# A two-layer attention and MLP kernel: dummy matmuls on a built-in constant, short ones behind the first transposes, b2 loaded later, new order lists

## The chip, the cores and the metric

The kernel runs on one core of a Trainium2 chip. The metric is the device time of one execution in microseconds, from the median of several runs; smaller is better. A profiled execution is a further run of the same program, for which every instruction's start and duration are recorded.

Five engines work side by side, each through its own list of instructions in order: TensorE (PE; its weight loads are shown as PEld), VectorE (DVE), ScalarE (ACT), GpSimd (POOL) and SyncE (SP), which here only issues DMAs. An engine that waits for a semaphore holds up everything behind the waiting instruction in its own list.

## The reference

The input `x` is one sequence of 2048 tokens of width 512. The same block, with the same weights, is applied twice:

```python
x = x + A(layernorm(x), wqkv, wo)              # linear attention, 32 heads of 16
x = x + B(layernorm(x), w1, b1, w2, b2)        # B normalises once more, then an MLP of width 1792
# A: q, k, v = x @ wqkv;  phi(t) = where(t > 0, t + 1, exp(t)) + 1e-6
#    kv = phi(k)^T v ;  z = sum over tokens of phi(k)
#    o = phi(q) kv / (phi(q) z + 1e-6) ;  result o @ wo
# B: gelu_tanh(layernorm(x) @ w1 + b1) @ w2 + b2
```

All inputs are bf16. The sum over tokens in `kv` and `z` means that no token's attention output is known before all 2048 tokens have been through the K projection.

## The kernel before, in words

**Tiling.** The 2048 tokens are four chunks of 512, each of four tiles of 128 (tile st = 4 * chunk + k). In layer 0 the chunks are taken in the order `C0=(3, 0, 1, 2)`, so tile 12 is the first one. For a tile the front does: statistics of the row (`stats`, `aggr`, or for tile 13 `sum` and `sq` on ScalarE), then `norm` (or `cen`, a subtraction of the mean, with the scale `ysc` applied afterwards), a transpose, and the K projection `K0_st` (four matmuls of 512 columns, L838), whose result goes through `exp`, `relu`, `min` and `phi` into `pk`. `G0_st` (L939) sums y^T phi(k) in four PSUM banks over all tiles. Q projections are `Q0_c_k` (L856, L869). Tiles 12 to 15 and tile 1 are transposed by TensorE (`PTA0_st`, L783, four matmuls of 128 columns, copied out of PSUM by ScalarE as `tcA0_st`, L793); all other tiles of layer 0 by DMA transposes that SP issues (`TA0_st`, L770).

**Loads.** `x0`, `x1` and `x2` are the first chunk's tiles 12, 13, and 14 with 15 (128, 128 and 256 KB). `wk0` and `wk1` are the halves of the K weights (256 KB each; `wk1` goes through ScalarE's queue, all others through SP's), `wq` the Q weights (512 KB). `xc0`, `xc1`, `xc2` are the chunks 0, 1, 2 (512 KB each, tiles 0 to 3, 4 to 7, 8 to 11; L638). `b1` and `b2` are biases; `b2` (128 KB) is broadcast over the partitions. `wv`, `wo`, `w1`, `w2` are issued by GpSimd once all of layer 0's first transposes are done.

**Order.** The program is a graph of named operations. `CONF["ORDER"]` holds one list of names for each engine, and the engine's instructions go out in exactly that order: `Scheduler.run` only ever takes the head of a list, `assign_waits` adds the semaphore waits that the graph's dependences need, and `play` emits them. `Scheduler.run` also carries a small model of times (how long a DMA takes, when the bus is free); it decides buffer slots, and the lists were settled with it. It doesn't reorder a list.

The lines that matter at the start are these:

```python
ones = G.op("dve", lambda e: e.memset(onesm[:], 1.0), 480, writes=["onesm"], ...)       # L641
def warm(e):                                                                            # L678
    for n in [D] * cf["N_WARM"] + [P]:
        ins = e.matmul(bank(wu, n), lhsT=onesm[:, 0:P], rhs=onesm[:, 0:n], start=True, stop=True)
```

`warm` is TensorE's first operation: seven dummy matmuls of 512 columns and one of 128, whose result nobody reads. It reads `onesm`, a tile that VectorE fills. The first entries of three lists of before are:

```
pe   warm PTA0_12 PTA0_13 K0_12 K0_13 PTA0_14 Q0_3_0 Q0_3_2 PTA0_15 K0_14 ... G0_14_0 Q0_3_3 PTA0_1 K0_0 K0_1 ...
dve  ones statsA0_12 aggrA0_12 cenA0_12 ... mink0_15 normA0_1 aggrA0_2 phik0_15 statsA0_8 normA0_2 ...
sp   x0 x1 wk0 x2 wq xc0 xc1 xc2 TA0_0 TA0_3 TA0_2 TA0_8 TA0_4 b2 TA0_6 TA0_7 TA0_5 TA0_10 TA0_11 TA0_9 b1 Tb1 ...
```

Of the kernel before, what the change touches and what calls it, by code (L numbers as in the profile page):

```python
# [6 lines left out]
BF16 = mybir.dt.bfloat16  # L7
# [3 lines left out]
P = 128  # L11
# [99 lines left out]
class Scheduler:  # L111
# [12 lines left out]
    def run(self):  # L124
# [14 lines left out]
        for _ in g.ops:  # L139
# [38 lines left out]
            if e == "sp" or o.sem is not None:  # L178
                if o.name[0] == "T":
                    o.end = max(at + o.lat, bus + 1000.0 if bus > at + 300.0 else 0.0)  # L180
                else:
                    bus = max(at + (1300.0 if at < 1400.0 else 1700.0 if e == "pool" else 900.0), bus) + o.nbytes
                    o.end = bus + o.lat
            else:
                o.end = at + dur + o.lat
# [79 lines left out]
def assign_waits(graph, order, sems, dma_sems):  # L265
# [10 lines left out]
    while len(done) < total:  # L276
        moved = False
        for e in ENGINES:
# [43 lines left out]
    C0=(3, 0, 1, 2), N_WARM=7, ZC=(0, 3), LQ='sp', N_HALF=1, N_K=4, N_Q=3, P_Z0=6.15, N_PB=1, N_PT=8, P_DEN=-50.43,  # L322
# [4 lines left out]
            "warm PTA0_12 PTA0_13 K0_12 K0_13 PTA0_14 Q0_3_0 Q0_3_2 PTA0_15 K0_14 G0_12_0 Q0_3_1 K0_15 G0_13_0 "  # L327
            "G0_14_0 Q0_3_3 PTA0_1 K0_0 K0_1 G0_15_0 K0_3 G0_0_0 K0_2 Q0_0_2 Q0_0_0 G0_1_0 K0_8 Z0_3 K0_4 G0_2_0 "
            "K0_6 G0_3_0 Q0_0_3 K0_7 K0_5 G0_4_0 K0_10 K0_11 Z0_0 K0_9 Q0_1_2 Q0_1_3 Z0_1 Q0_0_1 Q0_1_0 Z0_2 "
            "G0_5_0 G0_6_0 D0_0_3 D0_0_0 G0_7_0 Q0_1_1 D0_0_1 G0_8_0 D0_0_2 G0_9_0 G0_10_0 G0_11_0 G0_11_2 G0_11_1 "  # L330
            "D0_1_0 Q0_2_0 G0_11_3 KV0_0 KV0_1 D0_1_1 ZR0 KV0_2 KV0_3 Q0_2_1 D0_1_2 M0_0 M0_1 M0_2 M0_3 Q0_2_2 "
            "WO0_0_0 WO0_0_1 WO0_0_2 WO0_0_3 D0_1_3 WO0_1_0 WO0_2_0 WO0_3_0 Q0_2_3 WO0_4_0 WO0_7_0 WO0_6_0 PTB0_0 "
            "WO0_5_0 W10_0_5_0 W10_0_1_0 W10_0_9_0 W10_0_6_0 W10_0_2_0 W10_0_3_0 W10_0_12_0 W10_0_7_0 W10_0_0_0 "
            "W10_0_4_0 W10_0_13_0 W10_0_11_0 W10_0_8_0 W10_0_10_0 W20_0_0 W20_1_0 W20_0_7 W20_1_7 W10_0_9_1 "
            "W10_0_1_1 W10_0_7_1 W10_0_8_1 W10_0_5_1 W10_0_6_1 W10_0_12_1 W10_0_0_1 W10_0_13_1 W10_0_3_1 "
            "W10_0_11_1 W10_1_4_0 W10_1_13_0 W10_0_4_1 W10_1_11_0 W10_1_0_0 W10_1_3_0 W10_1_2_0 W10_0_2_1 "
            "W10_1_6_0 WO0_9_0 WO0_8_0 WO0_11_0 W10_1_5_0 W10_1_8_0 W10_1_10_0 WO0_10_0 W10_0_10_1 W10_1_1_0 "
            "W10_1_12_0 W10_1_7_0 W10_1_9_0 W20_7_0 W20_4_0 W20_7_7 W20_4_7 WO0_15_0 W20_5_0 W20_2_0 W20_5_7 "
# [24 lines left out]
            "reluq0_3_1 tcA0_1 expq0_3_1 expk0_0 reluk0_1 expk0_1 expq0_3_3 reluq0_3_3 normA0_8 expk0_3 expk0_2 "
            "normA0_6 reluk0_3 expq0_0_2 reluq0_0_2 reluq0_0_0 normA0_7 expk0_8 expk0_4 normA0_5 normA0_10 expk0_6 "
            "reluk0_6 expq0_0_0 expk0_7 expq0_0_3 reluk0_5 expk0_5 expk0_10 expk0_11 reluk0_11 reluk0_9 expk0_9 "
            "reluq0_1_2 expq0_1_2 expq0_1_3 expq0_0_1 reluq0_0_1 expq0_1_0 ln0_0_3 ln0_0_0 rec0_0_3 rec0_0_0 "
            "reluq0_1_1 ln0_0_1 rec0_0_1 expq0_1_1 ln0_0_2 rec0_0_2 ln0_1_0 b1c expq0_2_0 rec0_1_0 ln0_1_1 cpz0 "
            "rec0_1_1 cpm0_0 cpm0_1 cpm0_3 ln0_1_2 rec0_1_2 ln0_1_3 rec0_1_3 expq0_2_1 reluq0_2_1 expq0_2_3 "
# [159 lines left out]
def build_kernel(nc, A_x, A_wqkv, A_wo, B_x, B_w1, B_b1, B_w2, B_b2, out, conf=None, report=False):  # L528
# [5 lines left out]
    with ExitStack() as es:  # L534
# [48 lines left out]
        def bank(t, n=512):  # L583
            return ps[:, t.slot, 0:n]
# [62 lines left out]
        for h, q in enumerate(("sp", "act")):  # L647
            dma(q, lambda e, h=h: e.dma_start(wqkv[:, 2 * h:2 * h + 2, D:2 * D], wsrc[:, 2 * h:2 * h + 2, D:2 * D]), [f"wk_{h}"], prio=-99,
                name=f"wk{h}", kb=256, after=[ones] if q == "act" else ())
# [702 lines left out]
```

## Time and profile before

| | |
|---|---|
| runs | 331.65, 331.3, 328.13 us (median 331.3) |
| profiled execution, device time | 330.35 us |
| its span, first to last instruction | 328.6 us |
| PE busy | 322.0 us, 98% |
| DVE, ACT, POOL busy | 223.0 us (68%), 194.4 us (59%), 133.1 us (41%) |
| DMA | 20.37 MB, mean 62 GB/s |

The span is what the trace shows; 1.75 us of device time lie around it. A row of the timeline has the start, the duration, the engine, the line in the code, the operation, what it writes and reads, how many were merged into the row, and in brackets how long the engine had been idle before it and what ended that. A matmul's duration there includes its way through the array, so matmuls overlap; what a matmul costs TensorE is the distance from its start to the next one's.

### The profile page before, as it was taken

How to read it: one execution, taken by the hardware profiler on the slowest of the kernel's cores; microseconds unless marked ns; L12 is line 12 of the kernel's file. 1: busy time of each engine (PE TensorE's matmuls, PEld its weight loads, DVE VectorE, ACT ScalarE, POOL GpSimd, SP SyncE). 2: the span in 40 equal slices, each digit the busy share in tenths (PEclk: the TensorE clock that was granted, in tenths of full speed). 3: DMA queues.
4: the chain of work that ended last, by engine and by line, in shares of the span. 5: the costliest groups of instructions: out<-in, count | busy, mean ns of one | idle time of the engine just before them, and what ended most of it. 6: DMA issues, size and time to landing. Idle time of an engine off the chain costs nothing.

```text
span 328.6 us, 4769 instructions
## 1 busy us (share of the span) xinstructions
PE 322.0 (98%) x1716; PEld 159.1 (48%) x1716; DVE 223.0 (68%) x507; ACT 194.4 (59%) x334; POOL 133.1 (41%) x223
## 2 busy tenths in 40 slices
PE   7999999999999999999999999999999999999996
PEld 2444545476544444444444444448644444444444
DVE  4799599999794554575158899999989776100132
ACT  4898769783747055536984377878933452567200
POOL 3366646567447105533047725756903176000000
PEclk9999999999999999999999999999999999999999
DMA  6324593105404300312101110022044214200011
GB/s 231 152 49 98 121 358 149 18 16 97 49 0 66 80 16 3 64 32 48 34 16 32 35 32 0 2 49 50 18 96 99 48 33 97 64 0 2 16 48 64
DMA packets 47027, 20.37 MB, mean 62 GB/s; under 512 B 41948, under 2 KB 45532, under 8 KB 47004
## 3 DMA queue, kind: packets, MB, share of 16 engines
q1 hardware_dynamic: 45676, 15.09, 20.7%
q0 software_dynamic: 1056, 4.72, 4.1%
q8 instruction: 13, 0.21, 0.3%
q10 hardware_dynamic: 272, 0.26, 0.3%
q14 instruction: 10, 0.08, 0.1%
HBM read 8.00 MB, written 2.10 MB: 31 GB/s over the span
## 4 chain that ended last, share of the span: by engine, by line
PE 94%; DMA 2%; DVE 1%; ACT 1%; issue 0%; SPq 0%; ACTq 0%
PE ps L1119 30%; PE ps L1157 29%; PE ps L838 9%; PE ps L1087 8%; PE ps L856 5%; PE ps L971 4%; PE ps L939 3%; PE ps L869 2%; DMA wqkv<-in_A_wqkv_dram 1%; DMA t<-yb 1%; PE ps L1144 1%; PE ps L1063 1%; PE ps L1017 1%; PE ps L994 1%; PE ps L783 0%
## 5 line engine op out<-in xcount | busy, mean ns | idle before, releaser
L1125 ACT ACTIVATE gT<-ps,b1c 128x512 bf16<-128x512 f32 (+1 forms) x140 | 77.0, 601 | 53.8 <-PE ps L1119 53.3
L1119 PE MATMUL ps<-t,w 128*128 128x512 bf16 (+1 forms) x560 | 101.3, 336 | 0.4 <-issue 0.4
L1157 PE MATMUL ps<-w,gT 128*128 128x512 bf16 x434 | 97.3, 379 | 0.0
L1119 PEld LDWEIGHTS ps<-t,w 128*128 128x128 bf16 x560 | 54.6, 98 | 43.6 <-ACT t L793 1.2
L1157 PEld LDWEIGHTS ps<-w,gT 128*128 128x128 bf16 x434 | 42.5, 98 | 50.8
L808 ACT ACTIVATE eb<-ps 128x512 bf16<-128x512 f32 x56 | 32.5, 602 | 31.0 <-PE ps L838 25.6
L735 POOL TENSOR_TENSOR rstd<-veps,neghalf 128x1 f32<-128x1 f32 x64 | 37.8, 598 | 8.3 <-DVE veps L733 5.9
L1167 DVE TENSOR_TENSOR outb<-ps,xsb 128x512 bf16<-128x512 f32 x15 | 10.2, 683 | 40.2 <-PE ps L1157 38.7
L838 PE MATMUL ps<-wqkv,t 128*128 128x512 bf16 x128 | 33.6, 394 | 1.4 <-DMA t<-yb 0.7
L720 DVE BATCH_NORM_STATS2 stats<-xsb 128x6 f32<-128x512 f32 x48 | 32.0, 680 | 0.3
L1087 PE MATMUL ps<-gtb,t 128*128 128x512 bf16 x128 | 30.9, 379 | 0.0
L760 DVE TENSOR_SCALAR yb<-xsb,mv,rstd 128x512 bf16<-128x512 f32 x28 | 16.7, 602 | 13.6 <-POOL rstd L735 13.4
L733 POOL TENSOR_SCALAR veps<-mv 128x1 f32<-128x1 f32 x28 | 7.4, 276 | 43.7 <-DVE mv L722 43.0
L755 ACT ACTIVATE yb<-xsb,nmr,rstd 128x512 bf16<-128x512 f32 x20 | 15.7, 811 | 14.6 <-POOL nmr L752 14.6
L819 ACT ACTIVATE rb<-ps 128x512 bf16<-128x512 f32 x38 | 21.8, 601 | 0.2 <-PE ps L838 0.2
L821 DVE TENSOR_SCALAR eb<-eb 128x512 bf16<-128x512 bf16 x46 | 14.4, 325 | 10.1 <-ACT eb L808 10.0
L725 POOL TENSOR_SCALAR veps<-mv 128x1 f32<-128x1 f32 x32 | 8.8, 274 | 29.1 <-DVE mv L722 27.2
L838 PEld LDWEIGHTS ps<-wqkv,t 128*128 128x128 bf16 x128 | 12.3, 100 | 17.0 <-issue 1.7
L856 PE MATMUL ps<-wqkv,t 128*128 128x512 bf16 x80 | 20.3, 383 | 0.0
L1163 DVE TENSOR_TENSOR xsb<-ps,xsb 128x512 f32<-128x512 f32 x16 | 11.0, 688 | 13.2 <-PE ps L1157 13.1
L1087 PEld LDWEIGHTS ps<-gtb,t 128*128 128x128 bf16 x128 | 12.3, 98 | 15.1 <-DVE mv L722 0.5
L1104 POOL TENSOR_TENSOR xsb<-xsb,b2b 128x512 f32<-128x512 f32 x14 | 17.4, 1255 | 2.8 <-ACT yb L755 1.6
(103 smaller groups left out, 395.2 us busy)
## 6 DMA issues: line engine op xcount, KB each, us to landing
w<-in_B_w_dram POOLq DMA_DIRECT2D x4, 896.0 KB, 9.8
out_dram<-outb SPq DMA_DIRECT2D x15, 128.0 KB, 2.0
t<-in_A_x_dram SPq DMA_DIRECT2D x3, 512.0 KB, 7.3
t<-yb SPq DMA_TRANSPOSE x56, 2.5
wqkv<-in_A_wqkv_dram SPq DMA_DIRECT2D x1, 512.0 KB, 5.8
wo<-in_A_wo_dram POOLq DMA_DIRECT2D x1, 512.0 KB, 4.6
wqkv<-in_A_wqkv_dram POOLq DMA_DIRECT2D x1, 512.0 KB, 7.4
t<-t SPq DMA_TRANSPOSE x20, 2.5
```

The costliest lines, as they stand in the source:

```text
L720: G.op("dve", lambda e: e.bn_stats(stats[:, s.slot, :], src()), 620, reads=src_keys, writes=[k + "s"], tiles=[s, *src_tiles], prio=prio, n ...
L735: G.op("pool", lambda e: e.tensor_tensor(rstd[:, s.slot:s.slot + 1], veps[:, s.slot:s.slot + 1], neghalf[:], op=ALU.pow), 570, reads=[k + ...
L760: G.op("dve", lambda e: e.tensor_scalar(yb[:, y.slot, :], src(), stats[:, s.slot, 2:3] if by_act else mv[:, s.slot, 0:1], rstd[:, s.slot:s ...
L808: G.op("act", lambda e: e.activation(eb[:, et.slot, :], bank(bt), ACT.Exp, scale=factor()), 478, reads=[src_key, *more], writes=[f"e{tag}" ...
L819: G.op("act", lambda e: e.activation(rb[:, rt.slot, :], bank(bt), ACT.Relu, scale=factor()), 478, reads=[src_key, *more], writes=[f"r{tag} ...
L838: ins = e.matmul(bank(b), lhsT=yTa(yT)[:, dt, k * P:(k + 1) * P], rhs=wqkv[:, dt, D:2 * D], start=(dt == 0), stop=(dt == DT - 1))
L856: ins = e.matmul(bank(b), lhsT=yTa(yT)[:, dt, k * P:(k + 1) * P], rhs=wqkv[:, dt, 0:D], start=(dt == 0), stop=(dt == DT - 1))
L1087: ins = e.matmul(bank(wb), lhsT=yTa(pq)[:, kt, k * P:(k + 1) * P], rhs=gtb[:, kt, :], start=(kt == 0), stop=(kt == DT - 1))
L1104: G.op("pool" if on_pool else "dve", lambda e: e.tensor_tensor(xsb[:, st, :], xsb[:, st, :], b2b[:], op=ALU.add), 1120 if on_pool else 600 ...
L1119: ins = e.matmul(bank(b, n), lhsT=w1[:, dt, ft * P:(ft + 1) * P], rhs=yTa(yT)[:, dt, k0 * P:k1 * P], start=(dt == 0), stop=(dt == DT - 1))
L1125: G.op("act", lambda e, ft=ft, b=b, k0=k0, k1=k1, n=n: e.activation(gT[:, g.slot, ft * 512 + k0 * P:ft * 512 + k1 * P], bank(b, n), ACT.Ge ...
L1157: ins = e.matmul(bank(b), lhsT=gT[:, g.slot, ft * 512 + k * P:ft * 512 + (k + 1) * P], rhs=w2[:, ft, :], start=(ft == 0), stop=(ft == FT - 1))
```

## The change

- The dummy matmuls read a built-in constant 1.0 (one element for each partition, repeated by the access pattern) in place of `onesm`, so `warm` no longer waits for VectorE's fill. `N_WARM` goes from 7 to 8.
- Two groups of short dummy matmuls are new: `idle0_0` (four of 128 columns) behind `PTA0_12`, and `idle0_1` (three) behind `PTA0_13`. `PTA0_13` is made to come after `idle0_0`, and `K0_13` after the last dummy group.
- `b2` waits for all first transposes and stands behind them in SP's list; `b1` moves forward.
- The scheduler's model gets a table `LAND` with fixed times at which the first loads end. A load that stands in it gets that end whenever it is issued.
- All five lists are settled anew.

```diff
+                elif o.nbytes < 0:
+                    o.end = -o.nbytes
+                    bus = max(bus, o.end - 800.0)
...
-    C0=(3, 0, 1, 2), N_WARM=7, ZC=(0, 3), LQ='sp', N_HALF=1, N_K=4, N_Q=3, P_Z0=6.15, N_PB=1, N_PT=8, P_DEN=-50.43,
+    N_WARM2=1, N_IDLE=[4, 3], WK1=1,
+    LAND={'x0': 3210, 'x1': 3930, 'wk1': 5300, 'wk0': 6430, 'x2': 6950, 'wq': 8450, 'xc0': 9730, 'xc1': 11020, 'xc2': 12240},
+    C0=(3, 0, 1, 2), N_WARM=8, ZC=(0, 3), LQ='sp', N_HALF=1, N_K=4, N_Q=3, P_Z0=6.15, N_PB=1, N_PT=8, P_DEN=-50.43,
...
         "pe":
-            "warm PTA0_12 PTA0_13 K0_12 K0_13 PTA0_14 Q0_3_0 Q0_3_2 PTA0_15 K0_14 G0_12_0 Q0_3_1 K0_15 G0_13_0 "
-            "G0_14_0 Q0_3_3 PTA0_1 K0_0 K0_1 G0_15_0 K0_3 G0_0_0 K0_2 Q0_0_2 Q0_0_0 G0_1_0 K0_8 Z0_3 K0_4 G0_2_0 "
+            "warm PTA0_12 idle0_0 PTA0_13 idle0_1 K0_12 K0_13 PTA0_14 Q0_3_0 Q0_3_2 K0_14 PTA0_15 G0_12_0 Q0_3_1 "
+            "K0_15 Q0_3_3 G0_13_0 G0_14_0 PTA0_1 K0_0 G0_15_0 K0_1 K0_3 G0_0_0 K0_2 Q0_0_2 Q0_0_0 G0_1_0 K0_8 Z0_3 "
...
         "act":
+            "wk1 sumA0_13 tcA0_12 sqA0_13 tcA0_13 expk0_12 reluk0_12 tcA0_14 expk0_13 reluk0_13 reluq0_3_0 "
+            "expq0_3_0 expq0_3_2 tcA0_15 expk0_14 reluk0_14 yscA0_15 expk0_15 reluk0_15 normA0_3 reluq0_3_2 "
+            "expq0_3_1 tcA0_1 expk0_0 reluq0_3_1 expk0_1 reluk0_1 normA0_8 reluk0_3 expk0_3 expk0_2 expq0_3_3 "
...
         "dve":
+            "ones statsA0_12 aggrA0_12 cenA0_12 vepsA0_12 negA0_13 cenA0_13 yscA0_12 statsA0_14 aggrA0_14 cenA0_14 "
+            "vepsA0_14 statsA0_15 mink0_12 aggrA0_15 yscA0_14 phik0_12 vepsA0_15 cenA0_15 yscA0_13 mink0_13 "
+            "statsA0_0 phik0_13 aggrA0_0 minq0_3_0 statsA0_1 statsA0_3 aggrA0_1 aggrA0_3 normA0_0 mink0_14 "
+            "statsA0_2 phik0_14 mink0_15 statsA0_8 normA0_1 phik0_15 aggrA0_2 phiq0_3_0 statsA0_6 aggrA0_8 "
+            "normA0_2 minq0_3_2 aggrA0_6 phiq0_3_2 mink0_0 phik0_0 statsA0_4 statsA0_10 mink0_1 aggrA0_4 phik0_1 "
...
         "sp":
-            "x0 x1 wk0 x2 wq xc0 xc1 xc2 TA0_0 TA0_3 TA0_2 TA0_8 TA0_4 b2 TA0_6 TA0_7 TA0_5 TA0_10 TA0_11 TA0_9 b1 "
-            "Tb1 TB0_1 TB0_2 TB0_3 TB0_5 TB0_4 TB0_7 TB0_6 TP0_2_0 TP0_2_1 TP0_2_3 TP0_2_2 TB0_8 TP0_3_3 TA1_0 "
+            "x1 x2 wk0 x0 wq xc0 TA0_0 xc1 b1 TA0_3 xc2 TA0_2 TA0_8 TA0_4 TA0_6 TA0_7 TA0_5 TA0_10 TA0_11 TA0_9 b2 "
+            "Tb1 TB0_1 TB0_2 TB0_3 TB0_7 TB0_4 TB0_5 TB0_6 TP0_2_0 TP0_2_1 TP0_2_3 TP0_2_2 TP0_3_3 TA1_1 TB0_9 "
...
-            busy = 0.0 if transpose else kb * 1024 / 330.0
+            busy = 0.0 if transpose else -cf["LAND"][name] if name in cf["LAND"] else kb * 1024 / 330.0
...
-        def warm(e):
-            for n in [D] * cf["N_WARM"] + [P]:
-                ins = e.matmul(bank(wu, n), lhsT=onesm[:, 0:P], rhs=onesm[:, 0:n], start=True, stop=True)
+        def run_idle(e, sizes):
+            one = nc.const_aps.tensor(1.0, [P, D], BF16)
+            for n in sizes:
+                ins = e.matmul(bank(wu, n), lhsT=one[:, 0:P], rhs=one[:, 0:n], start=True, stop=True)
             return ins
-        G.op("pe", warm, cf["N_WARM"] * 427 + 107, reads=["onesm"], writes=["warm"], tiles=[wu], prio=-300, name="warm", n=cf["N_WARM"] + 1)
+        def idle(name, sizes, after=(), writes=()):
+            return G.op("pe", lambda e: run_idle(e, sizes), sum(sizes) / 1.2, writes=["warm", *writes], tiles=[wu], prio=-300, name=name,
+                        n=len(sizes), after=after)
+        idle("warm", [D] * cf["N_WARM"] + [P] * cf["N_WARM2"])
...
-                    tr = transpose_pe(y, ykey, yT, k, f"yT0_{st}", pr, f"A0_{st}", True)
+                    wait = [held] if held else ()
+                    tr = transpose_pe(y, ykey, yT, k, f"yT0_{st}", pr, f"A0_{st}", True, wait)
+                    held = idle(f"idle{n}_{k}", [P] * cf["N_IDLE"][k], [G.writer[f"yT0_{st}p"]]) if n == 0 and k < 2 else None
...
-                    dma("sp", lambda e: e.dma_start(b2b[:], bass.AP(B_b2.tensor, B_b2.offset, [[0, P], [1, D]])),
-                        ["b2b"], prio=-79, name="b2", kb=128, after=[tr])
...
-                pk = attn_k(0, c, k, yT, pr + 3, by)
+                pk = attn_k(0, c, k, yT, pr + 3, by, [G.writer["warm"]] if n == 0 and k == 1 else ())
...
         late("wo", "wo", wo[:], A_wo.rearrange("(dt p) c -> p dt c", p=P), -87, 512, trs)
+        dma("sp", lambda e: e.dma_start(b2b[:], bass.AP(B_b2.tensor, B_b2.offset, [[0, P], [1, D]])),
+            ["b2b"], prio=-79, name="b2", kb=128, after=trs)
```

`transpose_pe` and `attn_k` only pass their new argument `after` on to the graph. `WK1=1` leaves `wk1`'s wait as it was. In `WAY`, `TA1_5` goes from "dma" to "pe"; layer 1's first transposes are built by `transpose`, which doesn't ask `WAY`, and no `PTA1` stands in any list, so the entry changes nothing.

## The prediction

> **What bounds the kernel now.** I read the page first (busy shares, then the chain that ended last), then the timeline of TensorE for the first 31 us, then the timelines of the engines that feed it.
>
> ```profile
> PE 322.0 (98%) x1716; PEld 159.1 (48%) x1716; DVE 223.0 (68%) x507; ACT 194.4 (59%) x334; POOL 133.1 (41%) x223
> ...
> PE 94%; DMA 2%; DVE 1%; ACT 1%; issue 0%; SPq 0%; ACTq 0%
> ```
>
> TensorE is the bound, 94% of the chain. So I took the start-to-start distances of its matmuls and looked for what exceeds the usual 216 ns (512 columns). After 11 us only 2.8 us are lost in all: 0.88 before `K0_6` (30.66 us), 0.78 before `D0_0_3` (45.59), 0.55 before `W10_0_5_0` (65.61), 0.19 before `K0_1` (19.87), the rest small. What the start loses is therefore never made up, beyond these few places.
>
> TensorE's start:
>
> ```profile
> 1.51 3.27 PE L680 MATMUL ps<-onesm 128*128 128x512 bf16 x8 [1.51 <-DVE onesm L641]
> 4.59 1.32 PE L783 MATMUL ps<-idp,yb 128*128 128x128 bf16 x8
> 6.52 3.57 PE L838 MATMUL ps<-wqkv,t 128*128 128x512 bf16 x8 [0.61 <-DMA wqkv<-in_A_wqkv_dram]
> 9.88 0.63 PE L783 MATMUL ps<-idp,yb 128*128 128x128 bf16 x4
> 10.31 2.18 PE L856 MATMUL ps<-wqkv,t 128*128 128x512 bf16 x8
> ...
> 18.59 0.39 PE L783 MATMUL ps<-idp,yb 128*128 128x128 bf16 x4
> ...
> 30.66 0.59 PE L838 MATMUL ps<-wqkv,t 128*128 128x512 bf16 x2 [0.71 <-DMA t<-yb]
> ```
>
> `warm`, the transposes of tiles 12 and 13, then `K0_12` and `K0_13`: eight matmuls in 6.52 to 9.88, 427 ns each, half speed. The trace's record of the full clock begins at 10.89; from there the distance is 216 ns. `K0_12` waits for `wk0`, not for its tile. 18.59 is `PTA0_1`, 30.66 is `K0_6`, which waits for `TA0_6`.
>
> The two stretches of 3.41 us before 10.89, and the last 8.6 us:
>
> ```profile
> 4.06:7.48 3.42, 2.72 (x14) 1.28 (x13) 1.84 (x7) 2.51 (x6) 0.81 (x2) 1.00 1.03 346
> 7.48:10.89 3.41, 3.41 (x13) 1.48 (x11) 2.49 (x9) 1.60 (x3) 0.74 (x2) 1.00 1.03 418
> 320.00:328.60 8.60, 6.03 (x42) 3.92 (x40) 2.23 (x4) 0.00 (x0) 0.00 (x0) 0.98 0.19 61
> ```
>
> PE's busy time follows the comma. A stretch 80% busy did not raise the clock, one fully busy did. The record lasts 317.44 us, 93 times 3.413, and ends at 328.32, 2.3 us after the last matmul (hence 0.98 in the last row). I estimate from it: the clock is decided every 3.41 us; a full busy step raises it, a step mostly idle drops it.
>
> SP and VectorE:
>
> ```profile
> 0.80 0.40 SPq L642 DMA_DIRECT2D t<-in_A_x_dram  x1
> 1.25 0.41 SPq L644 DMA_DIRECT2D t<-in_A_x_dram  x1
> 1.72 0.43 SPq L648 DMA_DIRECT2D wqkv<-in_A_wqkv_dram  x1
> 2.19 0.47 SPq L644 DMA_DIRECT2D t<-in_A_x_dram  x1
> ...
> 3.17 1.84 SPq L638 DMA_DIRECT2D t<-in_A_x_dram  x3
> 15.86 1.30 SPq L770 DMA_TRANSPOSE t<-yb  x1
> ```
>
> ```profile
> 3.23 0.69 DVE L720 BATCH_NORM_STATS2 stats<-t 128x6 f32<-128x512 bf16 x1 [1.78 <-DMA t<-in_A_x_dram]
> ...
> 6.97 0.69 DVE L720 BATCH_NORM_STATS2 stats<-t 128x6 f32<-128x512 bf16 x1 [0.92 <-DMA t<-in_A_x_dram]
> ...
> 17.71 0.41 DVE L760 TENSOR_SCALAR yb<-t,mv,rstd 128x512 bf16<-128x512 bf16 x1
> ...
> 18.44 0.69 DVE L720 BATCH_NORM_STATS2 stats<-t 128x6 f32<-128x512 bf16 x1
> ```
>
> All nine loads are issued by 5.0 us; the first transpose only at 15.86. They land in the trace at 3.21 (`x0`), 3.93 (`x1`), 6.21 (`wk1`), 6.43 (`wk0`), 6.95 (`x2`), 8.45 (`wq`), 9.73, 11.02, 12.24 (the chunks): in order of issue on SP's queue. 3.23 is `statsA0_12`, at once behind `x0`; 6.97 `statsA0_14`, behind `x2`; 17.71 `normA0_1`, 18.44 `statsA0_8`.
>
> **Step 1, x0 in fourth place.** The table `LAND` repeats these landings (but for `wk1`) as facts, so the settled SP list could put the issues anywhere, and it did: `x1 x2 wk0 x0 wq xc0 TA0_0 xc1 b1 TA0_3 xc2`. The list is what SP plays. `x0` takes the place from which `x2` landed at 6.95, with the same 1024 KB moved by then. Lower bound: if all of `wk1` (256 KB; at the pace of 768 KB between 3.93 and 6.95, 1.0 us) comes behind it, 5.95. I take 6.95. `PTA0_12` came 1.36 after `statsA0_12`, so it starts at 6.97 + 1.36 = 8.33, not 4.59. Behind it TensorE runs 4 x 107 ns, `idle0_0` 4 x 107, `PTA0_13` 4 x 107, `idle0_1` 3 x 107 = 1.61 us: `K0_12` at 9.94 (its tile's copy would be there at 9.59, as 1.26 after `PTA0_12` before). Before 6.52: **+3.4 us**.
>
> **Step 2, the dummies.** Without the wait they begin near 0.9 (VectorE's own first row is at 0.97) and last 8 x 427 + 107 ns = 3.5 us, to 4.4. Then TensorE idles to 8.33. From 8.33 it is busy without a break, so the clock rises between one and two steps later, 11.7 to 15.2, middle 13.45: cold work from 9.94 to 13.45 costs half, 1.75, against (10.89 - 6.52) / 2 = 2.2 before. Gain 0.4 in the middle, +-0.85 by where the steps fall; bounds 2.2 gained, 0.4 lost. The spread of the runs shown, 328.13 to 331.65, is of this size.
>
> **Step 3, the chunks behind transposes.** `xc1` now stands behind `TA0_0`, `xc2` behind `TA0_3`, and SP waits there. `TA0_3` waits for ScalarE's `normA0_3`. ScalarE is without idle time from 10.6 to 20.9, so I shift it: `K0_12` and `K0_13` cold end at 9.94 + 8 x 0.427 = 13.36, then `PTA0_14`, `tcA0_14` at 13.9 (0.68 after its transpose cold, less warm); before, `normA0_3` ended 7.61 after `tcA0_14` began, with as many operations between: 21.5. `TA0_0` (`normA0_0` on VectorE, about 18.9 by the same shift) is done by then; `xc1` and `b1` go in between. `TA0_3` issues for 1.19, `xc2` at 22.7. Its landing: at least 2.95 (`b1`'s 1.70 from issue to landing, plus 1.25 for 512 KB), at most 4.35 (`b2`, 128 KB behind a transpose, 3.41; plus 0.94 for 384 KB more). I take 4.0, near `b2`, the likeliest row: 26.7.
>
> `statsA0_8` needs `xc2`, and in the new VectorE list `normA0_1` stands behind it. `PTA0_1` needs `normA0_1`, and TensorE stops there; what stands before `PTA0_1` is the same work as before and ends near 21.9. `PTA0_1` starts 0.62 + 0.41 + 0.06 behind 26.7: 27.8, not 18.59. **+9.2 us**, which contains steps 1 and 2. VectorE idles some 6 us, ScalarE (`tcA0_1` is next but two) as long. Behind it VectorE is 1.1 us ahead of TensorE, as against 0.15 before, so I count no second wait; `TA0_2` lands 5.4 after 26.7, `K0_2` asks for it at 6.8.
>
> **Step 4, b2.** Before, `b2` held `TA0_6` by 0.58 of issue and made its landing 3.3 instead of 2.4; that is `K0_6`'s 0.88, which goes. `K0_1`'s 0.19 goes as `G0_15_0` now precedes it. **-1.1**. `b2` is needed by `b20_1` long after; GpSimd's loads, issued after all transposes, move with TensorE.
>
> **Step 5, the clock again.** TensorE is idle from 21.9 to 27.8, so one step of 3.41 is at least 86% idle. That drops the clock, as after the last matmul; it rises 3.4 to 6.8 after 27.8. Half of 5.1: **+2.5** (1.7 to 3.4; nothing if it stays up).
>
> The page "TensorE: Matmul & The Clock Gate" of the Trainium skill, section "Seeing it yourself", shows a clock that fell 5.2 us after the last matmul. By that a 5.9 us break barely drops it, and the sum would be that without step 5; this trace's 2.3 us speaks for the drop.
>
> The other list changes I cost at nothing: the same operations, with only 2.8 us of losses to gain or double.
>
> **Sum**, against the profiled execution (330.35, within 0.95 of the median 331.3): 330.35 + 9.2 - 1.1 + 2.5 = **341.0 us**. Its own range: 341.0 - 1.0 - 0.85 - 1.05 = 338.1, to 341.0 + 0.85 + 0.35 + 0.85 = 343.0.
>
> **Rivals.**
> - *The clock stays up in the break*: 338.5. Decided by whether the clock drops sooner than 5.9 us after a matmul; the end of the trace speaks against it, but that is also the end of the program. 0.20.
> - *Only x0 is late*: xc2 lands before VectorE asks. It would have to be issued by 17; its issue follows `TA0_3`'s, which stood at 18.2 even before. 330.35 + 3.4 - 0.4 - 1.1 = 332.3, no measurable difference. 0.10.
> - *Faster: the loads land as they were*, because place in the queue doesn't set landing. Then `K0_12` starts at 6.5 with the clock up: -2.2 - 1.1 = 327.1. It decides if `x0` still lands by 3.9 (`K0_12` can follow 1.36 + 1.26 later, at 6.5) and no chunk is held. Against it: landings follow the issues in every row. 0.07.
> - *More waits behind the break*: `wo` is now GpSimd's fifth load instead of its first; the fifth landed at 52.3, and `M0_0`, which needs it, stood at 55.1. Its cover is 2.8 us; if `b2` and the transposes slow the loads by twice that, 2.8 us are added: 343.8. 0.08.
>
> **Numbers.** My forecast 0.55. 336.5 to 343.0 takes in it and the first rival down to a `xc2` that lands early; outside are 0.10 + 0.07 + 0.08 and little else. About 1% is what a measurement of this kernel can tell from no change: faster 0.07, same 0.10, slower 0.83.
>
> **What the changed profile would show.** Step 1: `statsA0_12` near 7, `K0_12` near 9.9. Step 2: `warm` from 0.9. Step 3: an `xc2` issue near 22.7, VectorE idle before `statsA0_8` for a DMA, `PTA0_1` near 27.8. Step 4: no wait before `K0_6`. Step 5: matmuls 427 ns apart behind 27.8. The forecast is wrong if the loads' issues stand together at the start, or if VectorE meets no idle time before `statsA0_8`.

## The result, and the profile after

The changed kernel takes **341.28 us** (median of four runs, 341.14 to 341.54); the kernel before, with a fourth run beside it, 329.73 us (328.13 to 331.65). The ratio is 1.035, with an interval of 1.027 to 1.042: slower. The profiled execution took 341.14 us with a span of 339.4; before it was 330.35 and 328.6, so 10.8 us are to be found.

The busy shares and the chain that ended last, of the kernel after:

```profile
PE 322.1 (95%) x1692; PEld 160.0 (47%) x1724; DVE 223.0 (66%) x507; ACT 193.4 (57%) x334; POOL 134.7 (40%) x223
...
PEclk9997999999999999999999999999999999999999
...
PE 87%; DVE 5%; ACT 3%; DMA 2%; POOL 1%; issue 1%; SPq 0%
```

PE's busy time is the same (322.1 against 322.0 us); its share of the chain fell from 94% to 87%. So TensorE has hardly more work, it waits more. The 7 in the clock's row is the slice from 25.5 to 33.9 us, in which the clock was down for a while.

SP's issues, from the timeline of the kernel after:

```profile
0.79 0.87 SPq L650 DMA_DIRECT2D t<-in_A_x_dram  x2
...
2.18 0.47 SPq L648 DMA_DIRECT2D t<-in_A_x_dram  x1
3.17 0.51 SPq L644 DMA_DIRECT2D t<-in_A_x_dram  x1
18.43 1.30 SPq L781 DMA_TRANSPOSE t<-yb  x1
19.79 0.56 SPq L644 DMA_DIRECT2D t<-in_A_x_dram  x1
...
21.08 1.20 SPq L781 DMA_TRANSPOSE t<-yb  x1
22.33 0.58 SPq L644 DMA_DIRECT2D t<-in_A_x_dram  x1
```

2.18 is `x0`, in fourth place; it landed at 6.64. 3.17 is `xc0`. Then SP waits 15 us for `TA0_0`'s tile; `xc1` is issued at 19.79 and `xc2`, behind `TA0_3`, at 22.33.

VectorE and TensorE, from their timelines:

```profile
6.66 0.69 DVE L731 BATCH_NORM_STATS2 stats<-t 128x6 f32<-128x512 bf16 x1 [5.21 <-DMA t<-in_A_x_dram]
...
26.33 0.70 DVE L731 BATCH_NORM_STATS2 stats<-t 128x6 f32<-128x512 bf16 x1 [6.21 <-DMA t<-in_A_x_dram]
26.95 0.40 DVE L771 TENSOR_SCALAR yb<-t,mv,rstd 128x512 bf16<-128x512 bf16 x1
```

```profile
0.83 3.68 PE L687 MATMUL ps<-const-bfloat16-1.0 128*128 128x512 bf16 x9 [0.83 <-PEq L1350]
8.02 0.61 PE L794 MATMUL ps<-idp,yb 128*128 128x128 bf16 x4 [3.51 <-DVE veps L744]
...
9.59 3.60 PE L849 MATMUL ps<-wqkv,t 128*128 128x512 bf16 x8
...
19.52 1.89 PE L950 MATMUL ps<-pkb,yb 128*128 128x512 bf16 x8
27.40 0.61 PE L794 MATMUL ps<-idp,yb 128*128 128x128 bf16 x4 [5.99 <-DVE yb L771]
27.80 1.91 PE L849 MATMUL ps<-wqkv,t 128*128 128x512 bf16 x4
30.68 1.24 PE L849 MATMUL ps<-wqkv,t 128*128 128x512 bf16 x5
```

In brackets stands how long the engine had been idle. Both breaks begin at a load: VectorE's 5.21 us before `statsA0_12` (`x0`), and 6.21 us before `statsA0_8` (`xc2`, landed 26.31). 26.95 is `normA0_1`, which needs nothing of `xc2` but stands behind `statsA0_8` in the list; TensorE's 5.99 us before `PTA0_1` follow. `PTA0_1` starts at 27.40, not 18.59: **8.8 us**.

Two matmul rows carry the clock. Four matmuls in 1.91 us at 27.80 are half speed (some 427 ns apart); five in 1.24 us at 30.68 are full speed. The clock's record is full from 13.05 to 26.70, half to 30.12, full again to the end. The steps around the break, by columns PE, PEld, DVE, ACT, POOL, clock, DMA share, GB/s:

```profile
23.29:26.70 3.41, 0.00 (x0) 0.00 (x0) 0.37 (x1) 0.00 (x0) 0.00 (x0) 1.00 0.47 158
26.70:30.12 3.42, 2.72 (x10) 1.31 (x11) 3.13 (x11) 0.97 (x2) 1.50 (x5) 0.50 0.02 5
```

A step without any matmul dropped the clock; the next one, busy for 2.72 of 3.42 us, raised it. So the half clock lasted one step, and cost 1.35 us: 1.15 in single distances of 0.1 us and more, 0.2 in `PTA0_1`'s short matmuls.

What TensorE waits for behind 31 us (in total, how often, longest, in us):

```profile
PE ps L1074 <- DVE zb L1011: 1.0, 1, 1.0
PE ps L1005 <- DVE gtb L995: 0.9, 1, 0.9
PE ps L931 <- DVE pkb L836: 0.6, 1, 0.6
PE ps L1130 <- ACT gT L1136: 0.3, 1, 0.3
```

These are `D0_0_0`, `KV1_3`, `Z0_1` and `W10_1_4_0` (the MLP's first matmuls on chunk 1, whose last transpose is `TB0_6`; at 93.48). By start-to-start distances they lose 1.17, 1.08, 0.72 and 0.43 us; `M1_0` loses 0.24. Before, `KV1_3`, `Z0_1` and `W10_1_4_0` lost nothing; the D group lost 0.78, `M1_0` 0.12. `Z0_1` waits for `phik0_5`, whose `mink0_5` the new VectorE list puts behind `mink0_10`, `zs0_0`, `minq0_0_0` and `phik0_10`; `KV1_3` for `gt1_3`, which stands behind `pz1_1_2` (1.5 us). `W10_1_4_0` goes on when the DMA transpose `TB0_6` has landed (93.17); it took 3.95 us instead of 2.56.

**The balance**: `PTA0_1` +8.8; the half clock behind it +1.35; `K0_6` and `K0_1` without their waits -1.07; `Z0_1` +0.72; the D group +0.39; `KV1_3` +1.08; `K0_10` +0.15; `M1_0` +0.12; `W10_1_4_0` +0.43; `W10_0_5_0`, whose wait of 0.55 is gone, -0.55; the rest, in parts too small to name, -0.6. The sum is 10.8.

### The profile page after: what moved, and what is told of

It is laid out like the page before. It is cut to its first block, busy times and chain, and to the rows that moved or that the text cites. A ratio compares the mean times of both kernels' runs of the same rounds, so it can differ in the third digit from the quotient of the medians.

```text
span 339.4 us, 4758 instructions
## 1 busy us (share of the span) xinstructions
PE 322.1 (95%) x1692; PEld 160.0 (47%) x1724; DVE 223.0 (66%) x507; ACT 193.4 (57%) x334; POOL 134.7 (40%) x223
## 4 chain that ended last, share of the span: by engine, by line
PE 87%; DVE 5%; ACT 3%; DMA 2%; POOL 1%; issue 1%; SPq 0%
PE ps L1130 28%; PE ps L1168 27%; PE ps L849 8%; PE ps L1098 8%; PE ps L867 3%; PE ps L950 3%; PE ps L982 3%; DMA t<-in_A_x_dram 2%; PE ps L880 2%; ACT eb L819 1%; PE ps L1155 1%; ACT rb L830 1%; PE ps L794 1%; POOL lr L1050 1%; DVE eb L832 1%
## 5 line engine op out<-in xcount | busy, mean ns | idle before, releaser
L1136 ACT ACTIVATE gT<-ps,b1c 128x512 bf16<-128x512 f32 (+1 forms) x140 | 76.1, 602 | 52.3 <-PE ps L1130 51.6
L746 POOL TENSOR_TENSOR rstd<-veps,neghalf 128x1 f32<-128x1 f32 x64 | 37.1, 594 | 7.9 <-DVE stats L722 5.7
L744 POOL TENSOR_SCALAR veps<-mv 128x1 f32<-128x1 f32 x28 | 9.5, 345 | 53.8 <-DVE mv L733 51.6
L771 DVE TENSOR_SCALAR yb<-xsb,mv,rstd 128x512 bf16<-128x512 f32 x28 | 15.4, 570 | 8.3 <-POOL rstd L746 7.7
L1062 POOL TENSOR_TENSOR t<-t,rr 128x512 bf16<-128x512 bf16 x7 | 8.2, 1178 | 26.6 <-DVE rr L1058 11.3
```

The costliest lines, as they stand in the source:

```text
L746: G.op("pool", lambda e: e.tensor_tensor(rstd[:, s.slot:s.slot + 1], veps[:, s.slot:s.slot + 1], neghalf[:], op=ALU.pow), 570, reads=[k + ...
L1136: G.op("act", lambda e, ft=ft, b=b, k0=k0, k1=k1, n=n: e.activation(gT[:, g.slot, ft * 512 + k0 * P:ft * 512 + k1 * P], bank(b, n), ACT.Ge ...
```

## The experiments

The theory: the order of SP's list alone makes the time, by `x0` (step 1) and by the chunks behind the transposes (step 3); the dummies, `b2` and the other lists move it by 1 or 2 us. The rivals: the new lists of the compute engines cost it, or the dummies, or the clock.

### The loads first again (`loads_first`)

```diff
-    x1 x2 wk0 x0 wq xc0 TA0_0 xc1 b1 TA0_3 xc2 TA0_2 ...     # sp, of after
+    x0 x1 wk0 x2 wq xc0 xc1 xc2 TA0_0 b1 TA0_3 TA0_2 ...
```

> The changed kernel with only SP's list mended at its head: x0 x1 wk0 x2 wq xc0 xc1 xc2 TA0_0 b1 TA0_3 TA0_2, all loads ahead of the first transpose and x0 first. My theory (x0's place and the chunks behind transposes are the whole loss): K0_12 near 6.5 behind wk0, no break before PTA0_1, no wait before K0_6; 327.5 to 331 us, so not slower than the kernel before. Rival theory (the new lists of the other engines or the dummies cost the time): still above 335 us, with K0_12 at 6.5.

Measured: 330.39 us (median of ten, 329.82 to 333.34), 1.005 of before (1.002 to 1.009), where before had a median of 328.69 over 19 runs. 10.9 of the 12.6 us by which after lies above that median come back through the place of a few names in one list. In its timeline both breaks are gone:

```profile
6.42 1.89 PE L849 MATMUL ps<-wqkv,t 128*128 128x512 bf16 x8
...
16.44 0.39 PE L794 MATMUL ps<-idp,yb 128*128 128x128 bf16 x4
```

`K0_12` and `K0_13` run at full speed from 6.42 (the clock's record is full from 5.69), and `PTA0_1` stands at 16.44, 2.15 us earlier than in the profile of before. All the same the kernel isn't faster than before, it is 0.5% slower, where "not slower" was expected. The 2.15 us are a head start against that one profile, in which the clock rose late; in a second profile of before (`before_a`, below) `PTA0_1` stands at 16.20. The waits of `loads_first` behind 11 us say where it goes:

```profile
PE ps L1074 <- DVE zb L1011: 1.0, 1, 1.0
PE ps L849 <- DMA t<-yb: 0.9, 1, 0.9
PE ps L1005 <- DVE gtb L995: 0.9, 1, 0.9
PE ps L931 <- DVE pkb L836: 0.6, 1, 0.6
```

Three of the four are those of after: they belong to the new lists, not to the late loads. The second is `K0_2`, which waits for `TA0_2`; that transpose took 4.09 us (an instruction fetch began 1.98 us behind its issue; more on this below).

### Only x0, only the chunks (`x0_first`, `chunks_first`)

```diff
-    x1 x2 wk0 x0 wq xc0 TA0_0 xc1 b1 TA0_3 xc2 TA0_2 ...     # sp, of after
+    x0 x1 wk0 x2 wq xc0 TA0_0 xc1 b1 TA0_3 xc2 TA0_2 ...     # x0_first
+    x1 x2 wk0 x0 wq xc0 xc1 xc2 TA0_0 b1 TA0_3 TA0_2 ...     # chunks_first
```

> The changed kernel with x0 x1 wk0 x2 at the head of SP's list, but xc1 still behind TA0_0 and xc2 behind TA0_3. My theory (two separate losses): K0_12 near 6.5; TA0_3 issued near 18.2 as before, xc2 near 19.5, landing 4.0 later at 23.5 (as 22.33 to 26.31 in the changed kernel), PTA0_1 near 24.6 instead of 27.4: 338.3 us. Rival theory (x0's place is the whole loss): 331 us or less.

> The changed kernel with xc1 and xc2 ahead of TA0_0, but x1 x2 wk0 x0 left as it is. My theory: K0_12 stays near 9.6, but TensorE goes on at 21.4 with PTA0_1 instead of 27.4 (6.0 less) and the clock doesn't drop (1.15 less): 334.0 us. Rival theory (the chunks' place is the whole loss and x0's is hidden): 330 us or less.

Measured: `x0_first` 338.8 us (four runs, 337.11 to 339.81; ratio 1.029, 1.023 to 1.034), `chunks_first` 336.22 (334.99 to 337.61; 1.023, 1.017 to 1.028). Their starts, the first of `x0_first`, the second of `chunks_first`:

```profile
6.76 3.28 PE L849 MATMUL ps<-wqkv,t 128*128 128x512 bf16 x8
...
24.77 0.61 PE L794 MATMUL ps<-idp,yb 128*128 128x128 bf16 x4 [6.51 <-DVE yb L771]
```

```profile
8.14 0.61 PE L794 MATMUL ps<-idp,yb 128*128 128x128 bf16 x4 [3.63 <-DVE veps L744]
9.71 3.35 PE L849 MATMUL ps<-wqkv,t 128*128 128x512 bf16 x8
...
21.11 0.39 PE L794 MATMUL ps<-idp,yb 128*128 128x128 bf16 x4
```

`x0` in its old place gives `K0_12` at 6.76, and the break before `PTA0_1` is there all the same, since SP still waits for two transposes before it issues `xc2` (landed 23.68). With the chunks in front instead, `K0_12` is late at 9.71 and there is no break. Against `loads_first` the late chunks alone cost 8.4 us and the late `x0` alone 5.8. Together they cost 10.9, not 14.2: a start that is 3 us late runs into the same stop before `PTA0_1`, and part of it would have been spent waiting there. `x0_first` came out near its forecast (338.3, with `PTA0_1` at 24.6; it starts at 24.77), `chunks_first` 2.2 us above its own (334.0): in its profile (334.99) `K0_2` loses 1.10 us to a slow `TA0_2` (4.09 us) and `W10_1_4_0` 0.56 to a slow `TB0_6` (4.08 us), of which more below. In `x0_first` the idle time is 6.51, in after 5.99, and the clock was down for two steps (23.22 to 30.05), not one.

### The break filled with matmuls (`break_filled`)

After, with 27 dummy matmuls ahead of `PTA0_1`, so that TensorE is busy while it waits:

```diff
-    ... G0_13_0 G0_14_0 PTA0_1 K0_0 ...
+    ... G0_13_0 G0_14_0 fill PTA0_1 K0_0 ...
+        def fill_fn(e):
+            one = nc.const_aps.tensor(1.0, [P, D], BF16)
+            for n in [D] * 27:
+                ins = e.matmul(bank(fu, n), lhsT=one[:, 0:P], rhs=one[:, 0:n], start=True, stop=True)
+            return ins
```

> The changed kernel with 27 more dummy matmuls of 512 columns put in ahead of PTA0_1, which fill 5.8 us of the 6.0 us in which TensorE waits for the late chunk. Theory (the break costs the clock one step of 3.41 us at half speed): the clock record has no half-speed step at 26.7, the matmuls behind PTA0_1 stand 216 ns apart from the first one, and the time is 1.15 us under the changed kernel's 341.2, 340.1 us. Rival (the half speed there is covered by VectorE's and ScalarE's backlog): 341.2 us, the 1.15 us come back as waits.

Measured: 341.85 us (340.67 to 342.08), 1.039 of before (1.035 to 1.043): no gain over after, where 340.1 was expected. Yet the clock did what was expected. The same two steps, and the timeline:

```profile
23.29:26.70 3.41, 3.41 (x18) 1.52 (x16) 0.00 (x0) 0.00 (x0) 0.00 (x0) 1.00 0.80 166
26.70:30.12 3.42, 2.55 (x16) 1.21 (x16) 2.96 (x10) 1.28 (x3) 1.09 (x3) 1.00 0.00 0
```

```profile
21.42 5.85 PE L1190 MATMUL ps<-const-bfloat16-1.0 128*128 128x512 bf16 x26
...
28.14 0.40 PE L794 MATMUL ps<-idp,yb 128*128 128x128 bf16 x4 [0.87 <-DVE yb L771]
```

The clock stays at 1.00 and the matmuls behind `PTA0_1` are 216 ns apart. From the start of `PTA0_1` to that of `W20_1_0`, some 55 us later, it takes 54.28 us and not 55.44, so 1.16 of the 1.35 is won. It is lost again at three places, and at each the trace has a DMA transpose into which an instruction fetch falls (see below). `xc2` landed at 27.05 instead of 26.31, while `TA0_3`, which stands before it on SP, took 4.75 us. `W10_0_6_1` waits 0.48 us; it starts 0.05 us behind the landing of `TB0_3`, which took 4.06. `W11_0_8_1` waits 1.08 us, which the profile puts down to nothing ("issue"); it starts 0.09 us behind the landing of `TB1_3`, which SP issued 2.26 us behind a slow `TB1_2` (3.36 us), and 1.23 behind it in after. So the half clock as a cost of some 1 us is shown where it arises; in the total it isn't seen.

### All code edits with the old lists (`old_lists`)

The dummies, `LAND` and `b2` behind all transposes, with the five lists of before, in which only the new names are put in place:

```diff
-    warm PTA0_12 PTA0_13 K0_12 ...                              # pe, of before
+    warm PTA0_12 idle0_0 PTA0_13 idle0_1 K0_12 ...
-    ... TA0_8 TA0_4 b2 TA0_6 TA0_7 TA0_5 TA0_10 TA0_11 TA0_9 b1 ...   # sp, of before
+    ... TA0_8 TA0_4 TA0_6 TA0_7 TA0_5 TA0_10 TA0_11 TA0_9 b2 b1 ...
```

> All edits of the changed kernel outside the lists (dummies on the constant, the two idle groups, b2 after all transposes), but the lists of before, with idle0_0 and idle0_1 put in and b2 behind TA0_9. My theory: K0_12 at 6.5 with the clock already full or within 1 us of it, PTA0_1 0.8 to 2.2 us earlier than 18.59, no wait before K0_6 (0.9): 327.1 to 328.3 us, and a narrower spread than 328.1 to 331.65. Rival theory (the dummies do nothing for the clock): 329.3 us, by b2 alone.

Measured: 330.46 us (median of ten, 329.02 to 331.67), 1.004 of before (1.002 to 1.007). A gain was expected (327.1 to 328.3 us). In its profile (329.02 us) the start is as expected, the clock full from 4.46 and `K0_15` done at 14.63 instead of 16.18. Of the waits, `Z0_1` and `KV1_3` lose nothing, so they do come with the new lists. But `W10_1_4_0`, at some 80 us, waits 1.20 us (`TB0_6` took 4.07), which it didn't before, and `K0_5` 0.50 (`TA0_5` took 3.16; what slowed that one stays open). Two runs were made to find which edit brings this.

### The dummies alone, b2 alone (`dummies_only`, `b2_only`)

```diff
-    warm PTA0_12 PTA0_13 K0_12 ...                     # pe, of before
+    warm PTA0_12 idle0_0 PTA0_13 idle0_1 K0_12 ...     # dummies_only
-    ... TA0_8 TA0_4 b2 TA0_6 TA0_7 TA0_5 TA0_10 TA0_11 TA0_9 b1 ...
+    ... TA0_8 TA0_4 TA0_6 TA0_7 TA0_5 TA0_10 TA0_11 TA0_9 b2 b1 ...   # b2_only, else before
```

> The kernel before with the dummies alone (constant, eight long ones, idle0_0 and idle0_1), its lists and b2 where they were. Theory (the dummies raise the clock by 7.6 us at the latest, where before it depends on where the steps fall): never above 329, median 328.3 us, ratio 1.00 or a little under, with the upper tail of before gone. Rival (front gains are lost again further on, as in the kernel with all edits under the old lists, 330.5): 329.5 to 330.5 us, ratio above 1.00, K0_15 done near 14.6 but the end no earlier than before.

> The kernel before with b2 behind all first transposes in SP's list, nothing else. Theory (b2 holds TA0_6 and so K0_6): no wait before K0_6, 0.9 us less: ratio 0.997. Rival (the next wait takes it): ratio 1.00, a new wait of 0.5 us or more at K0_5 or at the first operations of the MLP.

Measured, against a median of before of 328.28 over 29 runs (327.71 to 330.52): `dummies_only` 329.41 (twelve runs, 328.65 to 330.26), ratio 1.001 (0.9995 to 1.003); `b2_only` 328.76 (twelve, 327.29 to 330.07), ratio 1.000 (0.997 to 1.002). Neither can be told from before. The gains that were expected (nothing above 329 us; a ratio of 0.997) didn't come, and in both the rival that a later wait takes them is what the profile shows. (`dummies_only` also has `warm` on the constant, with `N_WARM` 8, and the table `LAND`; its `b2` stands as in before.)

The dummies do what they say: the clock is full from 3.58 and `PTA0_1` is done at 16.86, 2.1 us earlier than in the first profile of before, whose clock rose late (10.89). And they give it back:

```profile
PE ps L1129 <- ACT gT L1135: 1.7, 1, 1.7
PE ps L848 <- DMA t<-yb: 0.7, 1, 0.7
PE ps L1073 <- DVE zb L1010: 0.6, 1, 0.6
```

The first line is `W10_1_4_0` (1.84 us by distances). The gelu named there had long been done; what came last is the DMA transpose `TB0_6`, which took 4.70 us instead of 2.56.

In the profile of `b2_only` (330.07 us, its slowest run) `W10_1_4_0` waits too, 2.31 us, with `TB0_6` at 5.17. So the dummies aren't needed for that wait.

`b2_only` takes `b2` from `TA0_6`, and `K0_6` still waits 0.77 us (0.88 before): without `b2` ahead of it `TA0_6` took 3.85 us. In `dummies_only`, with `b2` ahead, it took 3.27; in `old_lists`, without, 2.50. So `b2` ahead is enough to slow that transpose, but isn't the only thing that does.

### What makes a transpose slow (copies, and `pad_eight`)

Three copies were run for further profiles, two of before and one of `dummies_only`, without an edit.

> The kernel before once more, for another profile. Its times lie in two groups, near 328.0 and near 330. Theory: what parts them is when the clock rises (before 7.5 us or near 10.9) and whether the 16 KB instruction fetch near 79 to 81 us delays the last sixteenth of TB0_6's transpose (a wait of 1.2 to 2.3 us before W10_1_4_0). Expected: clock late and no wait there, about 330.3 us; clock early and the wait, about 330; clock early and no wait, about 328.

> As the run before it, the same kernel: clock late and no wait before W10_1_4_0, about 330.3 us; clock early and the wait, about 330; clock early and no wait, about 328. A run that breaks this table tells against the theory.

> The kernel before with the dummies alone, once more for another profile. Theory: the clock is full by 7.6 us in any run, PTA0_1 done near 16.9, and the instruction fetch meets TB0_6 again (a wait of 1 us or more before W10_1_4_0), which is why its times stay at 329.4 and don't fall to 328.0. Rival: no such wait this time, and still 329 us or more.

Measured: 327.81 and 328.82 us for before, 330.42 for the dummies. In both copies of before `TB0_6` took 2.53 us and `W10_1_4_0` doesn't wait (2.56 and no wait in the first profile); in the copy of the dummies it took 4.82 and the wait is 1.96. So the wait stands in both profiles with the dummies and in none of the three of before. What differs is a packet of 16 KB on the queue that fetches instructions. The DMA view in the 1.1 us behind `TB0_6`'s issue, of before, and of `dummies_only`:

```profile
q1 hardware_dynamic: 441, 0.10, 47.9%
...
t<-yb SPq DMA_TRANSPOSE x1, 2.6
```

```profile
q1 hardware_dynamic: 411, 0.10, 43.9%
q8 instruction: 1, 0.02, 8.1%
...
t<-yb SPq DMA_TRANSPOSE x1, 4.7
```

In before the fetch comes 2.37 us behind the issue (2.37 and 2.46 in the copies), when the transpose has nearly landed; with the dummies 1.02 and 1.06 behind. Another such packet began 0.95 us behind `TA0_6` in `b2_only`, and none was near it in `dummies_only` and `old_lists`: with neither `b2` nor a fetch it took 2.50, with either over 3.2 us.

Against TensorE's work it comes some 0.9 us earlier with the dummies, which add eight matmuls: 14.85 and 14.89 us behind the start of `W10_0_5_0`, and 15.65 to 15.84 in the three profiles of before. That gave a test: before, with eight matmuls of 16 columns, some 0.2 us of work, and nothing else.

```diff
-    warm PTA0_12 PTA0_13 K0_12 ...
+    warm PTA0_12 PTA0_13 pad K0_12 ...
+        def pad(e):
+            for _ in range(8):
+                ins = e.matmul(bank(wu, 16), lhsT=onesm[:, 0:P], rhs=onesm[:, 0:16], start=True, stop=True)
+            return ins
```

> The kernel before with eight more matmuls of 16 columns behind PTA0_13, some 0.2 us of work in a stretch where TensorE waits for wk0 anyway; no other edit. Theory (the 16 KB instruction fetch near 79 us goes by how many instructions TensorE has passed, and the eight dummies that the change adds bring it forward into TB0_6's transpose): the fetch starts 0.9 us earlier against TensorE's own work, about 1.1 instead of 2.4 us behind TB0_6's issue; TB0_6 takes 4 us or more instead of 2.5; W10_1_4_0 waits 1 to 2 us; median 1.0 to 1.7 us above the kernel before, ratio 1.003 to 1.005. Rival (the fetch goes by something else, or the dummies' clock caused it): fetch 2.4 us behind TB0_6's issue as before, no wait before W10_1_4_0, ratio 1.000 to 1.001.

Measured: 330.82 us (twelve runs, 329.64 to 332.22), against 328.78 for before beside it (17 runs, 328.03 to 331.96); ratio 1.003 (1.0002 to 1.006). The DMA view behind its `TB0_6`, and TensorE's timeline:

```profile
q1 hardware_dynamic: 427, 0.10, 45.6%
q8 instruction: 1, 0.02, 7.0%
...
t<-yb SPq DMA_TRANSPOSE x1, 4.5
```

```profile
81.28 1.04 PE L1125 MATMUL ps<-t,w 128*128 128x256 bf16 x8
83.55 1.67 PE L1125 MATMUL ps<-t,w 128*128 128x512 bf16 x7 [1.24 <-ACT gT L1131]
```

The transpose was issued at 78.98, the fetch began at 80.10, 1.12 us behind, the transpose landed at 83.46, and `W10_1_4_0` starts at 83.55 (1.40 us lost). So eight more matmuls near 6 us make a transpose at 79 us slow, by moving the fetch 1.25 us nearer to its issue. The clock isn't needed for it: in this profile it rose at 10.50, as late as in the first one of before.

The 1.25 us have two parts. The fetch comes 0.70 us earlier against `W10_0_5_0` (14.95 instead of 15.65 us behind its start), and `TB0_6` is issued 0.55 us later (13.83 instead of 13.28), since `W10_0_5_0` itself no longer waits. Its 0.55 us before came from a fetch too: one that began 0.50 us behind `TB0_1`, which took 2.99 us and 2.42 in `pad_eight`. `b2_only` has the second part alone (fetch 15.80, issue 13.83), which is enough. So before isn't free of such delays; its fetch near 81 us falls into the next transpose, `TP0_2_0` (4.63 us), for which TensorE doesn't wait.

Which engine's instructions the packet holds isn't in the trace, but it goes with TensorE's list: in seven of the eight profiles with the old lists it begins behind the 493rd or 494th of TensorE's weight loads (behind the 498th in `old_lists`).

### The lists mended (`lists_mended`)

`loads_first`, with the two causes in VectorE's list taken away:

```diff
-    ... phiq0_0_3 mink0_10 zs0_0 minq0_0_0 phik0_10 mink0_5 phik0_5 mink0_9 ...
+    ... phiq0_0_3 mink0_5 zs0_0 phik0_5 mink0_10 phik0_10 minq0_0_0 mink0_9 ...
-    ... ga1_2_3 pz1_1_2 gt1_3 den1_1_1 ...
+    ... ga1_2_3 gt1_3 pz1_1_2 den1_1_1 ...
```

> The changed kernel with SP's list mended at its head, as in the run with all loads first, and two moves in VectorE's list: mink0_5 and phik0_5 back ahead of mink0_10, and gt1_3 ahead of pz1_1_2. Theory (the new lists' later waits are these two places): the waits before Z0_1 (0.72) and KV1_3 (1.09) shrink to under 0.3 each, time 1.0 to 1.6 us under 330.4. Rival (the waits have other causes): the waits stay or reappear nearby, 330.4 us.

Measured: 329.71 us (twelve runs, 328.9 to 331.06), 1.004 of before (1.002 to 1.006), not to be told from `loads_first`; 1.0 to 1.6 us less were expected. Its waits behind 11 us:

```profile
PE ps L1072 <- DVE zb L1009: 1.3, 1, 1.3
PE ps L1026 <- DVE kvb L1022: 1.2, 1, 1.2
PE ps L847 <- DMA t<-yb: 0.9, 1, 0.9
PE ps L1128 <- ACT gT L1134: 0.4, 1, 0.4
```

`Z0_1` and `KV1_3` no longer wait. `D0_0_0` behind the one loses 1.44 us (1.18 in `loads_first`), `M1_0` behind the other 1.32 (0.24). The reading is that TensorE is ahead of a longer chain in both places, so that mending one link moves the wait to the next. No version run here is faster than before by more than its interval; nearest are `b2_only` and `dummies_only`.

## Why the prediction was right, and where it wasn't

The forecast of 341.0 us and its direction were right (341.14 profiled). Point by point:

- **Step 1, x0 in fourth place**: held. `x0` landed at 6.64 (6.95 forecast), `PTA0_12` started at 8.02 (8.33), `K0_12` at 9.59 (9.94). The rival that place doesn't set landing fell: in `x0_first`, where `x0` stands first again, it landed at 3.80 and `K0_12` started at 6.76.
- **Step 2, the dummies**: held. They begin at 0.83, and the clock rose at 13.05 (13.45 forecast, between 11.7 and 15.2).
- **Step 3, the chunks behind transposes**: held, and carries the result. `TA0_3` 21.08 (21.5), `xc2` issued 22.33 (22.7), 3.98 us to landing (4.0), `PTA0_1` 27.40 (27.8), so +8.8 and not +9.2. The row that was taken for the unknown landing, a plain load behind a transpose, was a fitting one, but that it fits so closely is in part luck: the same load took 4.51 us in `x0_first` and 4.79 in `break_filled`, both above the forecast's upper bound of 4.35. `x0_first` and `chunks_first` show that steps 1 and 3 overlap, as the step says ("contains steps 1 and 2"): adding 8.4 and 5.8 would have been wrong by 3.3 us.
- **Step 4, b2**: the sum was right (-1.07 against -1.1), its cause only half told. `b2` ahead slows `TA0_6` to 3.2 us by itself, and so does an instruction fetch that falls into it; the profile of before had both (3.32 us, fetch 0.44 us behind). Taking `b2` away alone left 0.77 of `K0_6`'s 0.88 us in the profile of `b2_only`, where a fetch was there. In after neither is near, and it took 2.42. That the fetch is elsewhere comes with the other edits, which step 4 didn't count.
- **Step 5, the clock again**: the clock fell, but the term was mis-sized: 1.35 us measured, 2.5 forecast with 1.7 as its lower end. Two readings of the trace were too coarse. "A step mostly idle drops it": the step 19.88 to 23.29, busy 1.53 of 3.41 us, didn't, and only the empty one behind it did, so that the clock fell at 26.70, just before `PTA0_1`. "A full busy step raises it": one that was busy for 2.72 of 3.42 us did. So the wait was one step from 26.70, not 3.4 to 6.8 us from 27.4. The fall came 5.3 us after the last matmul at 21.4. The page "TensorE: Matmul & The Clock Gate" of the Trainium skill, section "Seeing it yourself", has 5.2 us in its example, and this break agrees. But it is no constant: the clock fell 2.3 us behind the last matmul at the end of before, 2.8 behind the first dummies of `break_filled` (4.07 to 6.89) and 5.0 in `x0_first`, each time at the end of a step. So the 2.3 us, on which the prediction leaned, weren't wrong, they were one place in a step. What it worked out from the Trainium skill's 5.2 us, a break that barely drops the clock, was near the truth: it dropped 0.7 us before the matmuls came back.
- **The other list changes "at nothing"**: wrong. They brought waits of 0.72 (`Z0_1`) and 1.08 (`KV1_3`), 0.39 more in the D group, 0.15 (`K0_10`) and 0.12 (`M1_0`): +2.46. The first two stand in every kernel run with the new lists as they are, whatever its start, and not in `old_lists`. The wait before `W10_0_5_0` that went (-0.55) and the one before `W10_1_4_0` that came (+0.43) go by the instruction fetches and not by the lists: the first is gone and the second there in `old_lists`, `dummies_only`, `b2_only` and `pad_eight` too. The reason given, that there were only 2.8 us of losses to gain or double, counts what an order has cost and not what another can cost.
- **The sum**: 9.2 - 1.1 + 2.5 = 10.6 was forecast, and 8.8 - 1.07 + 1.35 + 2.46 - 0.12 - 0.6 = 10.8 measured (2.46 for the lists, -0.12 for the two waits by fetches, -0.6 for the rest). That the total is nearer than its terms is luck: 1.15 too much for the clock and 0.4 too much for the start stand against 1.7 for what was put at nothing.
- **The rival of more waits behind the break**: its price of 2.8 us was of the right order, but the waits came from VectorE's order and a slow transpose, not from `wo`.

The dummies weren't taken out of the changed kernel alone; against the first profile of before they save 2.1 us at the start, of which nothing is left at the end (`dummies_only`). 1.84 us of it go to `W10_1_4_0`, through the fetch in `TB0_6`. Against `before_a`, whose clock rose early, they save nothing at the start (`PTA0_1` at 16.46 against 16.20).

## What to carry to other kernels

A load issued by an engine that also issues work waiting for others is only as early as what stands ahead of it in that list; a model that fixes when loads land will let a planner put them anywhere, so look at the issue times, and at what stands behind the first consumer on its own engine. A head start at the beginning is worth what the tightest chain further on leaves of it: list the waits on the bounding engine, and how close the next ones are, before counting it. Where two lists differ by some 1 us, settle it by distances in the trace at the place of the edit; the total also moves with where an instruction fetch falls.

## What was not expected of the hardware

- **Instruction fetches slow DMA transposes.** A packet of 16 KB on the instruction queue takes 0.9 to 1.7 us. In the fourteen profiles one began 0.4 to 2.1 us behind the issue of 84 of the transposes (`Tb1` not counted); all of them took 2.85 to 5.17 us. Of the 734 that had none from 2.5 us ahead of their issue to 4.0 us behind it, 97% took under 2.7 us, and none more than 3.27. In after `TA0_2` took 2.97 (fetch 0.49 behind), in `dummies_only` `TB0_6` 4.70 (1.02), in `b2_only` `TB0_6` 5.17 (1.97), in `break_filled` `TA0_3` 4.75 (2.29). At 2.37 and 2.46 behind there was no delay in `TB0_6` of before and of its copies, nor in `TB0_5` of after; but at 2.30 and 2.18 there was none either in `TA0_4` of before and of `b2_only`, so the edge isn't sharp. Every kernel here has such slow transposes, before too; they cost time only where TensorE waits for just that transpose. How a fetch slows one stays open: in `b2_only`, `TB0_6` had fifteen of its sixteen parts done at 79.48 us and the last at 82.18, but in `dummies_only` all sixteen were late, the first at 80.73, 3.87 us behind the issue (2.36 in before).
- **The spread of before** goes in part with the clock's first rise. `before_a` (clock full from 5.29) took 327.81 us and the first profile (from 10.89) 330.35, both without the wait at `TB0_6`. But `before_b`, whose short matmuls stand 55 ns apart from 5.36 on, took 328.82, so the clock isn't all of it: `K0_12` started at 6.60 there and at 6.11 in `before_a`, and `K0_6` waited 1.13 us and 0.77. Over the five profiles without the dummies `PTA0_1` starts at 16.20 to 18.59, over the five with them and `x0` in its old place at 16.35 to 17.14. So what the dummies take away is the late start. The twelve runs of `dummies_only` spread over 1.6 us, the 29 of before beside them over 2.8.
- **The clock's steps.** In steps of 3.41 us it rose behind ones busy 78% (`break_filled`, 0.07 to 3.48) and 80% (after, 26.70 to 30.12), and did not behind ones busy 75% and 80% (before, 0.65 to 4.06 and 4.06 to 7.48 by the busy column). So busy time as the profile shows it doesn't decide alone; in the second of these TensorE had short transposes and idle gaps, and with each matmul counted at its distance at half speed (427 ns for 512 columns) it was busy some 67%. Counted so, no step of up to 76% raised the clock (`x0_first` 74%, `pad_eight` 69%, `break_filled` 76% from 6.89 to 10.31), and those of 78% and more did (`dummies_only` 80%, `b2_only` 85%).
